# Seven-product block matmuls: partial sums kept in PSUM, remainders moved to VectorE, attention issued earlier

## The chip, the cores and the metric

The kernel runs on one core of a Trainium2 chip. The metric is device time in microseconds (us) of one launch. The core's engines are TensorE (PE in the profile; PEld is its weight load), VectorE (DVE), ScalarE (ACT), GpSimd (POOL) and SyncE (SP), which issues all of this kernel's transfers between HBM and the on-chip SBUF. TensorE writes its results only to PSUM, of which the kernel uses eight banks of 128 x 512 float32.

## The reference

An attention within chunks of 64 positions feeds two feed-forward layers, over 4608 tokens of width 512:

```python
scores = scale * q_c @ k_c.T            # 8 heads, chunks of 64 x 64
attn = softmax(scores); x = attn @ v_c  # -> (4608, 512)
g = x @ w_gate; val = x @ w_val         # 512 -> 1536 each
x = (g * sigmoid(g) * val) @ w_out      # 1536 -> 512
h = x @ w_in                            # 512 -> 2048
out = (h * sigmoid(1.702 * h)) @ w_out2 # 2048 -> 512
```

## The kernel before

**Tiling.** Tokens go in 9 blocks of 512 (NB = 9). The hidden columns of a layer are cut into passes: passes 0 and 1 hold six tiles of 128 columns each for layer 1, passes 2 and 3 eight tiles each for layer 2. A pass runs over all 9 blocks. Within a block the tiles of a pass come in groups: three groups of two tiles in passes 0 and 1 (27 groups a pass), two groups of four tiles in passes 2 and 3 (18 groups a pass); 90 groups in all.

**First matmuls.** A group multiplies with seven products instead of eight (the Strassen-Winograd scheme): sums and differences of quarters of the weights (`combos`) and of quarters of the block's tokens (`token_combos`) are made beforehand, and `group_products` adds and subtracts the seven results. Every float32 operand is held as a leading part and a remainder (`split`: ScalarE casts the leading part, another engine subtracts it for the remainder), so that each product of parts takes three matmuls (`mm3`). One product is 12 matmuls of 256 columns into one PSUM bank. Products are counted from 0. ScalarE copies the bank of product 0 (`copy(s1, m)`); VectorE adds the others into the sums with seven `tt` instructions, one each after products 1, 2, 3, 5 and 6 and two after product 4.

**Gate and second matmuls.** `gated` applies the sigmoid on ScalarE, multiplies on VectorE, and splits the result h into hh (cast on ScalarE) and hl (h minus hh; on GpSimd in pass 0, on VectorE after it). `second` multiplies hh and hl with a tile of the output weights, four quarters e = 0 to 3, three matmuls of 512 columns each, accumulated over the pass in four PSUM banks y0 to y3. A group's second matmuls wait in the list `pend` and are put between the products of the next group. `block_sum` adds a block's result to what earlier passes left in HBM.

**Pass 0** also makes the input: while it works on block b, `attend` computes the four attention units of block b + 1 (two sets of 32 small matmuls and four transposes on TensorE, reductions and the softmax on VectorE and ScalarE), and `x_made` turns their result xr (one buffer) into the seven token operands x (eight buffers, so all but one of the next block's wait for the last group of this block). Beside it the weights of pass 1 are unpacked and split (`group_to_dram`), mostly on GpSimd.

**Order.** The kernel writes out its own order: every instruction block is an `op` with an engine, an assumed duration and a priority (a planned time); `emit` plays this forward and, per engine, takes what could start first and, among those within 0.3 us (0.1 us on VectorE), the lowest priority. Each engine runs the resulting list in order and waits on semaphores for what an instruction needs. The plan assumes 1.2 us between the end of another engine's work and a TensorE instruction that needs it, and 0.3 us otherwise.

**PSUM.** Eight banks: y0 to y3; two of tag g, one s, one a. In pass 0 products alternate between the two g banks while s and a serve the attention; from pass 1 on products go round g, s, g, a.

Of the kernel before, what the change touches and what calls it, by code (L numbers as in the profile page):

```python
# [18 lines left out]
P = 128  # L19
# [120 lines left out]
def attention_two_moe_kernel(ctx: ExitStack, tc: tile.TileContext, q, k, v, wg, wv, wo, wi, wo2, out):  # L140
# [20 lines left out]

    nc = tc.nc
# [14 lines left out]
    FILL = 40  # L177
# [3 lines left out]
    for name, space in (("const", None), ("sb", None), ("ps", PSUM), ("dram", DRAM)):  # L181
        pool[name] = ctx.enter_context(tc.tile_pool(name=name, bufs=1, **({"space": space} if space else {})))
    ring = {tag: Ring(pool["sb"], tag, n) for tag, n in (
# [3 lines left out]
    ring.update({tag: Ring(pool["ps"], tag, n) for tag, n in (  # L187
        ("y0", 1), ("y1", 1), ("y2", 1), ("y3", 1), ("g", 2), ("s", 1), ("a", 1))})
# [53 lines left out]
    def mm3(o, ah, al, bh, bl, first, last):  # L242
        nc.tensor.matmul(o, ah, bh, start=first, stop=False)  # L243
        nc.tensor.matmul(o, ah, bl, start=False, stop=False)  # L244
        nc.tensor.matmul(o, al, bh, start=False, stop=last)  # L245
# [84 lines left out]
    def combos(t0, t1, prio):  # L330

        def half(i):
            return lambda ap: ap[:, i * 256:(i + 1) * 256]

        s1, s2, s3, s4 = [ring["st"].new([P, 256]) for _ in range(4)]
        a = half(0), half(1)
        yield t0, a[0]
        yield t0, a[1]
        tt(s1, t1, t1, ALU.add, 256, prio, "pool", a[0], a[1])
        tt(s2, s1, t0, ALU.subtract, 256, prio, "pool", of_b=a[0])  # L340
        yield s2, lambda ap: ap
        tt(s3, t0, t1, ALU.subtract, 256, prio, "pool", a[0], a[0])
        yield s3, lambda ap: ap
        yield s1, lambda ap: ap
        tt(s4, t0, s2, ALU.subtract, 256, prio, "pool", of_a=a[1])
        yield s4, lambda ap: ap
        yield t1, a[1]
# [77 lines left out]
    def attend(u, prio, load_prio, bufs=None, tags="sa"):  # L425
# [7 lines left out]
        s = ring[tags[0]].new([P, 512])  # L433

        def blocks(o, st, mv, of_o, of_st):

            for i in range(H):
                for r in (slice(0, CH), slice(CH, P)):
                    nc.tensor.matmul(o[r, of_o(i)], st[r, of_st(i)], mv[r, of_o(i)], start=True, stop=True)  # L439

        def cols(i):
            return slice(i * CH, i * CH + CH)

        op("pe", 1.2, lambda: blocks(s.ap, qb.ap, kb.ap, cols, cols), [qb, kb], [s], prio)
# [12 lines left out]

        pt = ring[tags[1]].new([P, 512])
# [8 lines left out]
        o = ring[tags[1]].new([P, 512])  # L467

        op("pe", 1.2, lambda: blocks(o.ap, vb.ap, e.ap, cols, cols), [vb, e], [o], prio)
        b = u // UPB  # L470
        if b not in xr:
            xr[b] = ring["xr"].new([P, KD, BT])
        ts = slice(u % UPB * P, u % UPB * P + P)
        copy(xr[b].part(lambda ap: ap[:, :, ts]), o, 512, prio, cut=lambda ap: ap.rearrange("p (a t) -> p a t", a=NP))


    def token_combos(xb, prio):
# [13 lines left out]
        return [(xb, b[0][0]), (xb, b[1][0]), (t2, same), (t3, same), (t1, same), (xb, b[1][1]), (t4, same)]  # L491
# [27 lines left out]
    m_tags = []  # L519

    def product(g, xs, i, prio):
        if not m_tags:
            m_tags.extend(["g", "g"] if prio < start[1][0] else ["g", "s", "g", "a"])
        m = ring[m_tags.pop(0)].new([P, 2, HT])
        w, x = W[g][i], xs[i]

        def fn():
            for var in range(2):
                for kk in range(2):
                    ks, cs = slice(kk * P, kk * P + P), kk  # L530
                    mm3(m.ap[:, var], w.ap[:, var, 0, ks], w.ap[:, var, 1, ks], x.ap[:, 0, kk], x.ap[:, 1, kk],
                        kk == 0, kk == 1)

        op("pe", GV, fn, [w, x], [m], prio)
        return m

    def group_products(g, xs, at, put):
# [4 lines left out]
        s1 = ring["s1"].new([P, 2, HT])  # L542
        u = ring["u"].new([P, 2, 2, HT])
        u2, u3 = [u.part(lambda ap, n=n: ap[:, n]) for n in range(2)]
        for i in range(7):
            at_i = at(i)
            m = product(g, xs, i, at_i)
            if i == 0:
                copy(s1, m, 512, at_i)
            elif i == 1:  # L550
                tt(q[0][0], s1, m, ALU.add, 512, at_i)
            elif i == 2:
                tt(u2, s1, m, ALU.add, 512, at_i)
            elif i == 3:
                tt(u3, u2, m, ALU.add, 512, at_i)
            elif i == 4:
                tt(q[0][1], u2, m, ALU.add, 512, at_i)
                tt(q[1][1], u3, m, ALU.add, 512, at_i)
            elif i == 5:
                tt(q[0][1], q[0][1], m, ALU.add, 512, at_i)  # L560
            else:
                tt(q[1][0], u3, m, ALU.subtract, 512, at_i)
            put(i)
        return c

    def gated(g, c, prio):

        hs = []
# [3 lines left out]
        for i, var in ([(0, 0), (1, 0)] if g.layer == 1 else [(i, var) for var in range(2) for i in range(2)]):  # L572
# [5 lines left out]
            if g.layer == 1:  # L578
# [4 lines left out]
                  h, 512, prio, "pool" if prio < start[1][0] else "dve")  # L583
            hs.append((hh, hl))
        return hs
# [50 lines left out]
    warm = ring["y0"].new([P, 512])  # L636

    def warm_up():
        for i in range(8):
            nc.tensor.matmul(warm.ap[:, :P], ident.ap, ident.ap, start=True, stop=True)  # L640

    op("pe", 3.6, warm_up, [ident], [warm], -99)
    for i in range(FILL):
        op("pe", 0.22, lambda: nc.tensor.matmul(warm.ap[:, :P], ident.ap, ident.ap, start=True, stop=True), [warm], [], 9999)
# [7 lines left out]
    for u in range(UPB):  # L652
# [4 lines left out]
        attend(u, -40 + 4 * u, -60 + u, bufs, (("s", "a"), ("g", "y2"), ("g", "y3"), ("y1", "y2"))[u])  # L657
# [4 lines left out]
    OW = {(0, 0, g0, 0): out_from_host(g0, 0, 0)}  # L662
    group_from_host(gs0[1], 2)
    for i in range(2):
        key = (0, 0, gs0[i], 1 - i)
# [18 lines left out]
    for p, (layer, gs) in enumerate(passes):  # L684
        jobs = spread(p)
        for b in range(NB):
# [3 lines left out]
            for j, g in enumerate(gs):  # L690
# [8 lines left out]
                c = group_products(g, xs, lambda i, tj=tj, step=step: tj + i * step / 7, put)  # L699
                if j == 0:  # L700
                    ys = [ring[f"y{e}"].new([P, BT]) for e in range(KD)]
                hs = gated(g, c, tj + step)
                for m, (hh, hl) in enumerate(hs):
                    for e in range(KD):
                        first, last = j == 0 and m == 0, j == len(gs) - 1 and m == len(hs) - 1

                        def fn(prio, g=g, m=m, hh=hh, hl=hl, e=e, first=first, last=last, ys=ys, p=p, b=b, layer=layer):
# [4 lines left out]
                            if last:  # L712
                                block_sum(p, b, ys, e, prio + 0.5)

# [63 lines left out]
```

## Time and profile before

| what | value |
|---|---|
| median of 3 runs | 1814.8 us (1814.05 to 1817.19) |
| profiled execution, its own time | 1817.76 us |
| its span, first to last instruction | 1815.7 us |
| TensorE busy in the span | 1745.7 us (96%) |
| VectorE, ScalarE, GpSimd busy | 1243.3, 703.7, 549.0 us |
| granted TensorE clock, mean share of full speed | 0.986 |

The profile comes from one execution. Matmuls overlap one another, so that a TensorE shown busy is not always one at its full rate; a stretch is better judged by how many matmuls it finished.

### The profile page before, as it was taken

The page shows a single profiled execution, that of the slowest core. Times are in us where ns is not written, and L with a number is a line of the kernel's source. Part 1 is how long each engine was busy: PE and PEld are TensorE (multiplying, and loading weights), DVE is VectorE, ACT ScalarE, POOL GpSimd, SP SyncE. Part 2 cuts the span into 40 slices and gives each one's busy share as a digit, 9 for nine tenths or more (in the row PEclk, how much of TensorE's full clock was granted, in tenths as well). Part 3 has the DMA queues.
Part 4 walks back from the last instruction along what each step waited for, and adds up shares of the span by engine and source line. Part 5 has one row for each costly group of instructions (what it writes and reads, how often), then busy time and mean ns, then how long its engine had stood idle before and what let it go on. Part 6 is the DMA issues. An engine that isn't in the chain of part 4 may idle for free.

```text
span 1815.7 us, 33814 instructions
## 1 busy us (share of the span) xinstructions
PE 1745.7 (96%) x13128; PEld 1581.0 (87%) x13128; DVE 1243.3 (68%) x1846; ACT 703.7 (39%) x1218; POOL 549.0 (30%) x594
## 2 busy tenths in 40 slices
PE   7869999998999999999999999999999999999998
PEld 7768888888988999999999998889888888888886
DVE  7988787888888567888888766555544455555554
ACT  5766455555554223333333233333222222222222
POOL 4775565566556033345434222200000000000000
PEclk9889999999999999999999999999999999999999
DMA  7457777777785988888888999966668667666664
GB/s 278 160 207 243 266 246 238 258 273 243 250 280 195 403 298 307 285 287 297 304 294 289 358 346 340 330 210 212 222 218 294 230 232 242 241 226 226 230 213 161
DMA packets 183918, 473.53 MB, mean 261 GB/s; under 512 B 19792, under 2 KB 46416, under 8 KB 183760
## 3 DMA queue, kind: packets, MB, share of 16 engines
q1 hardware_dynamic: 183760, 471.38, 75.4%
q8 instruction: 104, 1.70, 0.4%
q14 instruction: 54, 0.44, 0.1%
HBM read 336.56 MB, written 134.74 MB: 260 GB/s over the span
## 4 chain that ended last, share of the span: by engine, by line
PE 81%; DVE 9%; POOL 4%; issue 2%; DMA 2%; ACT 1%; SPq 0%; DVEq 0%; POOLq 0%; ACTq 0%
PE y L244 12%; PE y L243 12%; PE y L245 12%; PE g L243 9%; PE g L245 9%; PE g L244 9%; PE s L244 3%; PE s L245 3%; PE s L243 3%; PE a L244 3%; PE a L245 3%; PE a L243 3%; DVE h L236 2%; PE a L439 2%; DVE t L323 1%
## 5 line engine op out<-in xcount | busy, mean ns | idle before, releaser
L243 PE MATMUL g<-x,w 128*128 128x256 f32 x1640 | 470.3, 287 | 15.3 <-DVE c L236 7.5
L244 PE MATMUL g<-x,w 128*128 128x256 f32 x1640 | 465.6, 284 | 7.7 <-POOL x L236 7.4
L245 PE MATMUL g<-x,w 128*128 128x256 f32 x1640 | 465.0, 284 | 0.4 <-POOL w L236 0.4
L575 ACT ACTIVATE h<-c 128x512 f32<-128x512 f32 x252 | 156.6, 632 | 591.6 <-DVE c L236 585.5
L243 PEld LDWEIGHTS g<-x,w 128*128 128x128 f32 x1640 | 312.0, 190 | 33.0 <-DVE c L236 6.4
L244 PEld LDWEIGHTS g<-x,w 128*128 128x128 f32 x1640 | 311.8, 190 | 20.8 <-POOL x L236 9.0
L236 DVE TENSOR_TENSOR h<-h,c 128x512 f32<-128x512 f32 x360 | 289.1, 816 | 44.1 <-ACT h L575 40.3
L245 PEld LDWEIGHTS g<-x,w 128*128 128x128 f32 x1640 | 311.9, 190 | 0.6 <-POOL w L236 0.6
L227 ACT CAST hh<-h 128x512 fp32r<-128x512 f32 x252 | 154.5, 620 | 204.6 <-DVE h L236 100.8
L243 PE MATMUL y<-o,hh 128*128 128x512 f32 x576 | 227.6, 395 | 0.0
L245 PE MATMUL y<-o,hl 128*128 128x512 f32 x576 | 227.5, 395 | 0.0
L244 PE MATMUL y<-o,hh 128*128 128x512 f32 x576 | 227.3, 395 | 0.0
L236 DVE TENSOR_TENSOR hl<-h,hh 128x512 fp32r<-128x512 f32 x200 | 143.7, 726 | 70.1 <-ACT hh L227 68.4
L244 PE MATMUL y<-hl,o 128*128 128x512 f32 x432 | 173.7, 402 | 10.2 <-POOL hl L236 7.9
L243 PE MATMUL y<-hh,o 128*128 128x512 f32 x432 | 175.6, 407 | 4.4 <-ACT hh L227 4.4
L236 DVE TENSOR_TENSOR c<-u,g 128x512 f32<-128x512 f32 x174 | 114.2, 683 | 95.6 <-PE g L245 93.9
L245 PE MATMUL y<-hh,o 128*128 128x512 f32 x432 | 172.7, 400 | 0.0
L245 PEld LDWEIGHTS y<-o,hl 128*128 128x128 f32 x576 | 108.1, 188 | 26.1
L244 PE MATMUL s<-x,w 128*128 128x256 f32 x440 | 123.9, 282 | 0.0
L244 PE MATMUL a<-x,w 128*128 128x256 f32 x440 | 123.9, 282 | 0.0
L245 PE MATMUL s<-x,w 128*128 128x256 f32 x440 | 123.8, 281 | 0.0
L245 PE MATMUL a<-x,w 128*128 128x256 f32 x440 | 123.8, 281 | 0.0
(119 smaller groups left out, 3202.5 us busy)
## 6 DMA issues: line engine op xcount, KB each, us to landing
x<-x_dram SPq DMA_DIRECT2D x189, 512.0 KB, 5.6
o<-od_b SPq DMA_DIRECT2D x144, 512.0 KB, 4.9
o<-od_a SPq DMA_DIRECT2D x102, 512.0 KB, 5.3
x_dram<-x SPq DMA_DIRECT2D x63, 512.0 KB, 4.1
wd_b<-ws SPq DMA_DIRECT2D x56, 256.0 KB, 4.4
w<-wd_b SPq DMA_DIRECT2D x28, 512.0 KB, 6.3
raw<-in_moe_w_out SPq DMA_DIRECT2D x56, 255.8 KB, 4.1
wd_a<-ws SPq DMA_DIRECT2D x42, 256.0 KB, 4.1
```

What stands on the lines that cost most here:

```text
L227: op("act", act_us(n), lambda: nc.scalar.copy(out=dst.ap, in_=cut(src.ap)), [src], [dst], prio)
L236: lambda: e.tensor_tensor(out=dst.ap, in0=of_a(a.ap), in1=of_b(b.ap), op=by), [a, b], [dst], prio)
L243: nc.tensor.matmul(o, ah, bh, start=first, stop=False)
L244: nc.tensor.matmul(o, ah, bl, start=False, stop=False)
L245: nc.tensor.matmul(o, al, bh, start=False, stop=last)
L323: op("dve", dve_us(1.3 * n), lambda: nc.vector.scalar_tensor_tensor(out=t.ap.bitcast(I32), in0=t.ap, scalar=-4096 * up, in1=word(1).bitcas ...
L439: nc.tensor.matmul(o[r, of_o(i)], st[r, of_st(i)], mv[r, of_o(i)], start=True, stop=True)
L575: op("act", act_us(512), lambda h=h, i=i, var=var, by=by: nc.scalar.activation(out=h.ap, in_=of(var)(c[i].ap), func=AF.Sigmoid, scale=by), ...
```

## The change

Four things are changed together.

- `group_products` takes two PSUM banks for a group and issues some products on top of what stands in the bank: product 2 onto 0, product 4 onto 0 + 2, product 6 onto 3. The order of the products is changed (in `combos`, `token_combos`). ScalarE copies the bank after products 0, 2 and 4 (s1, u2, u3); VectorE adds or subtracts four times (after products 1, 4, 5 and 6). Product 2 must so wait until product 0 was read, and product 5, which overwrites the bank of product 4, until product 4 was copied. `pend` leaves room for second matmuls between products 4 and 5. In pass 0 all groups use banks ga and gb; later passes alternate with s and a.
- All remainders hl are subtracted on VectorE, in pass 0 too.
- The attention of the next block gets priorities that begin 22 us ahead of the block, 14 us apart (before: at the block's start, 12 us apart), and `x_made` 20 us ahead of its block (before: 12).
- Besides: y0 to y3 become two tiles ya, yb of two banks each; early attention units use other banks; `gated` takes the second half of the tokens first and makes a fourth h only when the first one's second matmuls are listed; the filler matmuls at the start go from 40 to 24.

```diff
-    FILL = 40
+    FILL = 24
-        ("w", 21), ("o", 3), ("x", 8), ("c", 3), ("s1", 1), ("u", 1), ("h", 2), ("hh", 3), ("hl", 3),
+        ("w", 21), ("o", 3), ("x", 8), ("c", 3), ("u", 3), ("h", 2), ("hh", 3), ("hl", 3),
-    ring.update({tag: Ring(pool["ps"], tag, n) for tag, n in (
-        ("y0", 1), ("y1", 1), ("y2", 1), ("y3", 1), ("g", 2), ("s", 1), ("a", 1))})
+    ring.update({tag: Ring(pool["ps"], tag, 1) for tag in ("ya", "yb", "ga", "gb", "s", "a")})
...
+        bank = [ring[t].new([P, 2, HT]) for t in (("s", "a") if p and n_groups[0] % 2 else ("ga", "gb"))]
...
+        for i, (k, goes_on) in enumerate(((0, 0), (1, 0), (0, 1), (1, 0), (0, 1), (0, 0), (1, 1))):
+            m, w, x = bank[k], W[g][i], xs[i]
...
+                            kk == var == 0 and not goes_on, kk == 1, skip_group_check=True)
...
             if i == 0:
                 copy(s1, m, 512, at_i)
             elif i == 1:
                 tt(q[0][0], s1, m, ALU.add, 512, at_i)
             elif i == 2:
-                tt(u2, s1, m, ALU.add, 512, at_i)
-            elif i == 3:
-                tt(u3, u2, m, ALU.add, 512, at_i)
+                copy(u2, m, 512, at_i)
             elif i == 4:
+                copy(u3, m, 512, at_i)
+                tt(q[1][1], u3, bank[1], ALU.add, 512, at_i)
+            elif i == 5:
+                tt(q[1][0], u3, m, ALU.subtract, 512, at_i)
+            elif i == 6:
                 tt(q[0][1], u2, m, ALU.add, 512, at_i)
-                tt(q[1][1], u3, m, ALU.add, 512, at_i)
-            elif i == 5:
-                tt(q[0][1], q[0][1], m, ALU.add, 512, at_i)
-            else:
-                tt(q[1][0], u3, m, ALU.subtract, 512, at_i)
...
-                  h, 512, prio, "pool" if prio < start[1][0] else "dve")
+                  h, 512, prio)
...
-        attend(u, -40 + 4 * u, -60 + u, bufs, (("s", "a"), ("g", "y2"), ("g", "y3"), ("y1", "y2"))[u])
+        attend(u, -40 + 4 * u, -60 + u, bufs, (None, None, "yb", "ya")[u])
...
-                    while len(pend) > n * (6 - i) // 7:
-                        pend.pop(0)(tj + (i + 0.5) * step / 7)
+                    while len(pend) > n * (7 - i - (i > 3)) // 8:
+                        pend.pop(0)(tj + (i + (i > 4) + 0.5) * step / 8)
...
-                        at = t + u * 12
+                        at = t - 22 + u * 14
...
-                        x_made(b + 1, start[p][b + 1] - 12)
+                        x_made(b + 1, start[p][b + 1] - 20)
```

## Rows read from the trace of the kernel before

**Rows 1.** The page's chain of work that ended last, by engine.

```profile
PE 81%; DVE 9%; POOL 4%; issue 2%; DMA 2%; ACT 1%; SPq 0%; DVEq 0%; POOLq 0%; ACTq 0%
```

**Rows 2.** Stages: start-up, pass 0 block 0, blocks 1-8, pass 1, passes 2-3.

```profile
core 0: us, PE busy (x) PEld busy (x) DVE busy (x) ACT busy (x) POOL busy (x), PEclk, DMA share, GB/s
0.00:34.50 34.50, 26.99 (x437) 25.26 (x437) 22.38 (x42) 17.80 (x33) 10.60 (x20) 0.97 0.78 283
34.50:125.30 90.80, 69.06 (x670) 61.13 (x669) 80.49 (x117) 65.05 (x126) 71.72 (x72) 0.84 0.52 183
125.30:616.60 491.30, 461.44 (x4334) 415.97 (x4333) 386.88 (x583) 265.00 (x433) 273.09 (x299) 0.99 0.75 258
616.60:1040.20 423.60, 421.56 (x2917) 391.56 (x2916) 344.67 (x479) 139.68 (x255) 158.34 (x157) 1.00 0.88 306
1040.20:1807.00 766.80, 766.66 (x4777) 687.11 (x4775) 407.55 (x627) 216.18 (x372) 35.30 (x48) 1.00 0.73 247
```

**Rows 3.** Same columns: one block of pass 1, one of pass 3.

```profile
663.30:709.90 46.60, 46.60 (x325) 43.49 (x324) 36.27 (x58) 17.45 (x32) 22.09 (x27) 1.00 0.86 287
1541.80:1584.10 42.30, 42.30 (x265) 37.94 (x264) 22.14 (x35) 10.62 (x19) 0.00 (x0) 1.00 0.69 235
```

**Rows 4.** TensorE's waits, blocks 1-8 of pass 0: total us, times, longest.

```profile
PE g L243 <- DVE c L236: 7.5, 7, 1.8
PE g L244 <- POOL x L236: 6.1, 5, 2.5
PE y L244 <- POOL hl L236: 5.3, 4, 1.9
PE y L243 <- ACT hh L227: 3.9, 4, 1.5
PE g L243 <- DVE u L236: 1.6, 2, 1.3
```

**Rows 5.** TensorE's waits in pass 1.

```profile
PE y L244 <- DVE hl L236: 2.0, 4, 0.6
```

**Rows 6.** VectorE by form, blocks 1-8 of pass 0: busy us, mean ns | idle before.

```profile
L236 DVE TENSOR_TENSOR h<-h,c 128x512 f32<-128x512 f32 x97 | 82.6, 866 | 8.6 <-ACT h L575 7.7
L236 DVE TENSOR_TENSOR c<-u,g 128x512 f32<-128x512 f32 x73 | 47.9, 682 | 29.8 <-PE g L245 29.6
```

**Rows 7.** VectorE by form, pass 1.

```profile
L236 DVE TENSOR_TENSOR hl<-h,hh 128x512 fp32r<-128x512 f32 x54 | 42.7, 790 | 0.7 <-ACT hh L227 0.3
```

**Rows 8.** VectorE by form, 1200 to 1800 us (passes 2 and 3, GpSimd idle).

```profile
L236 DVE TENSOR_TENSOR hl<-h,hh 128x512 fp32r<-128x512 f32 x115 | 77.9, 689 | 61.8 <-ACT hh L227 60.5
L236 DVE TENSOR_TENSOR h<-h,c 128x512 f32<-128x512 f32 x116 | 77.4, 688 | 16.4 <-ACT h L575 14.8
```

**Rows 9.** GpSimd by form, blocks 1-8 of pass 0.

```profile
L236 POOL TENSOR_TENSOR hl<-h,hh 128x512 fp32r<-128x512 f32 x48 | 67.1, 1405 | 97.5 <-ACT hh L227 95.7 <-issue 1.3
L236 POOL TENSOR_TENSOR x<-xr,x 128x512 fp32r<-128x512 f32 x29 | 42.7, 1481 | 1.4 <-DMA v<-in_v 1.2 <-ACT x L227 0.2
```

**Rows 10.** ScalarE by form, blocks 1-8 of pass 0.

```profile
L450 ACT ACT_TABLE_LOAD x22 | 28.2, 1283 | 0.4
...
L466 ACT COPY e<-a 128x512 f32<-128x512 f32 x27 | 15.7, 583 | 28.7 <-PE a L463 27.6 <-ACT h L575 0.6 <-DVE h L236 0.3
L227 ACT COPY s<-g 128x512 f32<-128x512 f32 x24 | 13.9, 579 | 5.8 <-PE g L245 5.7
```

**Rows 11.** Timeline, pass 0, a product that waits for a copy: start us, us.

```profile
128.31 0.66 PE L463 MATMUL a<-ident,e 128*128 128x128 f32 x4 [1.40 <-ACT xr L227]
...
130.00 0.28 PE L244 MATMUL g<-x,w 128*128 128x256 f32 x1
130.11 0.28 PE L245 MATMUL g<-x,w 128*128 128x256 f32 x1
130.24 0.58 ACT L227 COPY s<-g 128x512 f32<-128x512 f32 x1
...
130.87 0.39 PE L243 MATMUL g<-x,w 128*128 128x256 f32 x1 [0.48 <-ACT s L227]
```

**Rows 12.** Timeline of TensorE, an attention product of 32 small matmuls.

```profile
191.12 1.15 PE L439 MATMUL a<-e,v 64*64 64x64 f32 x32
192.20 0.39 PE L243 MATMUL g<-x,w 128*128 128x256 f32 x1
```

**Rows 13.** Timeline of TensorE in block 0, at a lower granted clock.

```profile
105.06 0.41 PE L244 MATMUL g<-x,w 128*128 128x256 f32 x1
105.27 0.41 PE L245 MATMUL g<-x,w 128*128 128x256 f32 x1
```

More of the change, by code (lines that the diff above doesn't have):

```diff
@@ L240, in split, with mm3 @@
         tt(lo, src, hi, ALU.subtract, n, prio, eng, of_a=cut, of_b=rd)
[L242 to L245, printed above, removed]
+    def mm3(o, ah, al, bh, bl, first, last, **kind):
+        nc.tensor.matmul(o, ah, bh, start=first, stop=False, **kind)
+        nc.tensor.matmul(o, ah, bl, start=False, stop=False, **kind)
+        nc.tensor.matmul(o, al, bh, start=False, stop=last, **kind)
     class Group:
@@ L432, in attend, with blocks @@
             load(b, src[u].rearrange("p h t -> p (h t)"), load_prio + 4 * (i > 1))
-        s = ring[tags[0]].new([P, 512])
-        def blocks(o, st, mv, of_o, of_st):
+        if both is None:
+            s = ring["s"].new([P, 512])
+        else:
+            both = ring[both].new([P, 2, 512])
+            s = both.part(lambda ap: ap[:, 0])
+        def blocks(o, st, mv):
             for i in range(H):
                 for r in (slice(0, CH), slice(CH, P)):
[L439 to L444, printed above, removed]
+                    cs = slice(i * CH, i * CH + CH)
+                    nc.tensor.matmul(o[r, cs], st[r, cs], mv[r, cs], start=True, stop=True)
+        op("pe", 1.2, lambda: blocks(s.ap, qb.ap, kb.ap), [qb, kb], [s], prio)
         m = ring["m"].new([P, H, 1])
@@ L456, in attend, with ps @@
             out=heads(e.ap), in0=heads(e.ap), in1=z.ap.to_broadcast([P, H, CH]), op=ALU.mult), [e, z], [e], prio)
-        pt = ring[tags[1]].new([P, 512])
+        def ps():
+            return ring["a"].new([P, 512]) if both is None else both.part(lambda ap: ap[:, 1])
+        pt = ps()
         def transposes():
@@ L466, in attend @@
         op("act", 0.59, lambda: nc.scalar.copy(out=e.ap, in_=pt.ap), [pt], [e], prio)
-        o = ring[tags[1]].new([P, 512])
-        op("pe", 1.2, lambda: blocks(o.ap, vb.ap, e.ap, cols, cols), [vb, e], [o], prio)
+        o = ps() if both is None else pt
+        op("pe", 1.2, lambda: blocks(o.ap, vb.ap, e.ap), [vb, e], [o], prio)
         b = u // UPB
@@ L490, in token_combos @@
         same = lambda ap: ap
-        return [(xb, b[0][0]), (xb, b[1][0]), (t2, same), (t3, same), (t1, same), (xb, b[1][1]), (t4, same)]
+        return [(xb, b[0][0]), (xb, b[1][0]), (t2, same), (t1, same), (t3, same), (t4, same), (xb, b[1][1])]
     X = {}
@@ L516, in x_to_dram, with group_products, fn @@
                 store(x_dram[1][:, b, i, c * 512:(c + 1) * 512], Buf(lambda s=s: s.ap.rearrange("p a t -> p (a t)"), None, None, s), [xd[1][b][i].part(None)], prio + i + 2)
[L519 to L537, printed above, removed]
+    n_groups = [0]
+    def group_products(g, xs, at, put, p):
+        n_groups[0] += 1
+        bank = [ring[t].new([P, 2, HT]) for t in (("s", "a") if p and n_groups[0] % 2 else ("ga", "gb"))]
         c = [ring["c"].new([P, 2, 2, HT]) for _ in range(2)]
         q = [[c[i].part(lambda ap, n=n: ap[:, n]) for n in range(2)] for i in range(2)]
[L542 to L545, printed above, removed]
+        s1, u2, u3 = [ring["u"].new([P, 2, HT]) for _ in range(3)]
+        for i, (k, goes_on) in enumerate(((0, 0), (1, 0), (0, 1), (1, 0), (0, 1), (0, 0), (1, 1))):
+            m, w, x = bank[k], W[g][i], xs[i]
+            def fn(m=m, w=w, x=x, goes_on=goes_on):
+                for var in range(2):
+                    for kk in range(2):
+                        ks = slice(kk * P, kk * P + P)
+                        mm3(m.ap[:, var], w.ap[:, var, 0, ks], w.ap[:, var, 1, ks], x.ap[:, 0, kk], x.ap[:, 1, kk],
+                            kk == var == 0 and not goes_on, kk == 1, skip_group_check=True)
             at_i = at(i)
-            m = product(g, xs, i, at_i)
+            op("pe", GV, fn, [w, x], [m], at_i)
             if i == 0:
@@ L566, in gated @@
     def gated(g, c, prio):
-        hs = []
         def of(var):
             return lambda ap: ap[:, :, var]
-        for i, var in ([(0, 0), (1, 0)] if g.layer == 1 else [(i, var) for var in range(2) for i in range(2)]):
+        for i, var in ([(1, 0), (0, 0)] if g.layer == 1 else [(i, var) for i in (1, 0) for var in range(2)]):
             h = ring["h"].new([P, 2, HT])
@@ L695, in put, with fn @@
                 def put(i, tj=tj, n=n, step=step):
-                    while len(pend) > n * (6 - i) // 7:
-                        pend.pop(0)(tj + (i + 0.5) * step / 7)
-                c = group_products(g, xs, lambda i, tj=tj, step=step: tj + i * step / 7, put)
+                    while len(pend) > n * (7 - i - (i > 3)) // 8:
+                        pend.pop(0)(tj + (i + (i > 4) + 0.5) * step / 8)
+                c = group_products(g, xs, lambda i, tj=tj, step=step: tj + (i + (i > 4)) * step / 8, put, p)
                 if j == 0:
-                    ys = [ring[f"y{e}"].new([P, BT]) for e in range(KD)]
-                hs = gated(g, c, tj + step)
-                for m, (hh, hl) in enumerate(hs):
+                    yab = [ring["y" + i].new([P, 2, BT]) for i in "ab"]
+                    ys = [yab[e // 2].part(lambda ap, e=e: ap[:, e % 2]) for e in range(KD)]
+                more, hs = gated(g, c, tj + step), []
+                hs.extend(next(more) for i in range(min(3, len(g.fs))))
+                for n in range(len(g.fs)):
                     for e in range(KD):
-                        first, last = j == 0 and m == 0, j == len(gs) - 1 and m == len(hs) - 1
-                        def fn(prio, g=g, m=m, hh=hh, hl=hl, e=e, first=first, last=last, ys=ys, p=p, b=b, layer=layer):
+                        first, last = j == 0 and n == 0, j == len(gs) - 1 and n == len(g.fs) - 1
+                        def fn(prio, g=g, n=n, hs=hs, more=more, e=e, first=first, last=last, ys=ys, p=p, b=b, layer=layer):
+                            m, hh, hl = hs[n]
                             key = (p, b, g, m)
@@ L713, in fn @@
                                 block_sum(p, b, ys, e, prio + 0.5)
+                            if e == KD - 1 and len(hs) < len(g.fs):
+                                hs.append(next(more))
                         pend.append(fn)
```

19 lines of the change are left out of this document (9 added, 10 removed).

## The prediction

> **What bounds the kernel now.** I read the chain of work that ended last, then a table of stages, then who TensorE waited for in each. The chain is TensorE's for 81% of the span, with VectorE at 9% and GpSimd at 4% [rows 1]; those 13% must lie somewhere in particular. The stages show where. In passes 2 and 3 TensorE is busy for 766.7 of 766.8 us, and in pass 1 for 421.6 of 423.6 [rows 2]. A block of pass 1 takes 46.6 us for its 324 matmuls, one of pass 3 takes 42.3 us for 264 [rows 3]; nine times 46.6 is 419.4, so pass 1 gives away about 4 us, and 18 times 42.3 is 761, so the last two passes give away almost nothing (the rest of their stretch is the second matmuls of the last group).
>
> Pass 0 is another matter. Blocks 1 to 8 take 491.3 us [rows 2]. Eight blocks of 46.6 are 372.8. An attention unit costs TensorE two products of 1.08 us (from the start of one to the start of what follows it) and transposes of at most 0.66 [rows 11, 12], some 2.6 with their overlap; 27 units, counted by their copies [rows 10], are 70. That is 443, so 48 us are lost there. TensorE is idle in 29.9 of them (491.3 - 461.4); the remaining 18 are slow restarts after a stop and matmuls at a lower clock, so that a microsecond of idle time costs about 1.6. In block 0, 21.7 us of 90.8 are idle at a clock of 0.84.
>
> So whatever the change does to VectorE in passes 1 to 3 can bring at most 4 us. What it can win lies in pass 0, and what it can lose lies in every pass, since there TensorE has no slack.
>
> **Sums in PSUM.** Each group loses three of seven VectorE additions and gains two ScalarE copies. At 0.682 us for an addition that reads PSUM [rows 6] and 0.579 for the copy [rows 10], the 24 groups of blocks 1 to 8 give VectorE back 72 x 0.682 = 49 us and cost ScalarE 48 x 0.579 = 28, on top of 265 of 491 (54%): it goes to about 64% of a shorter stretch.
>
> **Remainders on VectorE.** 48 subtractions leave GpSimd, which is relieved of 67 of 273 us [rows 2, 9]. On VectorE no row of pass 0 shows one. The bounds are 0.689 us, where GpSimd is idle [rows 8], and 0.866, what h x c with the same two SBUF inputs takes in pass 0 [rows 6]; pass 1 has this very instruction beside a working GpSimd at 0.790 [rows 7]. I take 0.83, nearer to pass 0's own row: 40 us. In return, 97 instructions h x c took 0.866 instead of 0.688 [rows 6, 8], 17 us of slowing beside a GpSimd busy for 56%; with a quarter less GpSimd work about 4 come back. VectorE's sum is -49 + 40 - 4 = -13: 374 us, in a stretch that I expect at about 466, so still 80%. The additions that read PSUM take 0.68 everywhere, so they aren't what GpSimd slows.
>
> The Trainium skill, "SBUF — State Buffer", section "Who interferes with whom", says that a VectorE instruction with two SBUF inputs and a GpSimd instruction that reads SBUF exclude each other for a whole instruction, whichever came first. The trace agrees in kind: 0.866 and 0.688 for the same form. If every moved subtraction stood behind one whole GpSimd instruction of 1.4 us, they would cost 67 us more and VectorE would have about 440 of 466 us to do; by the rows it is the 5 to 9 us already in the sum.
>
> **What this does to TensorE's waits in blocks 1 to 8** [rows 4]. For additions it waits 9.1 us (7.5 and 1.6) with two rotating banks. It keeps two banks, but a product now waits for one short reading instruction, half of the time on the less loaded ScalarE: I take 5 off (bounds 0 and 9). For x, made late on GpSimd at the change of block, 6.1: the attention is planned a third of a block earlier, and hl no longer stands between the x instructions of 1.48 us on GpSimd's queue: 5 off (0 and 6). For hl 5.3: VectorE needs 0.83 for GpSimd's 1.4 and has no queue of weight work ahead: 4 off (0 and 5). For hh 3.9: these fall where no product of the next block is ready, which an earlier x provides: 3 off (0 and 4). Together 17 of idle time, 27 us at 1.6. Against it stands the new direct wait of product 5 for the copy of product 4. A copy costs from the last matmul's start to the next product's start 130.87 - 130.11 = 0.76 us, where the next would have come after 0.12: 0.64 uncovered [rows 11]. By the new order two second matmuls stand in between. A product is 12 matmuls of 0.12, 1.42 us by the starts [rows 11]; 21 of them leave 16.8 of a block's 46.6 us for 24 second matmuls [rows 3], so one takes 0.70 and the two 1.4, and the wait is covered unless ScalarE is more than about 0.8 us late; a table load of 1.283 in front of it [rows 10] does that now and then. I charge 2 us. Blocks 1 to 8: -25 (bounds -48 and +10).
>
> **Block 0 and the start.** 6 subtractions less on a GpSimd that is busy for 71.7 of 90.8 us, three additions less per group on VectorE (80.5 of 90.8) [rows 2]. But two of the first four attention units now share the banks s and a one after the other, and the next block's first unit is planned ahead of this block's x. I take -3, between -10 and +8. Fewer fillers are priced at nothing: they fill idle time ahead of the first product; should the clock be lower when it starts, its 12 matmuls go at 0.21 us instead of 0.12 [rows 11, 13], 1 us a product.
>
> **Pass 1.** All its idle time, 2.0 us, is for hl behind a VectorE busy for 345 of 424 us [rows 2, 5]; 27 x 3 x 0.68 = 55 us less on VectorE: -2. **Passes 2 and 3:** nothing to win. The new wait is covered by four second matmuls (2.8 us) there, by two in pass 1: 0, at worst 63 x 0.64 = 40 us if nothing covers it. The two-bank tiles ya and yb make a block's first second matmul wait for two sums instead of one; a whole group of seven products (10 us) lies in between, which hides it. In the tail after 1807 us nothing changes.
>
> **Sum.** -25 - 3 - 2 = -30 us. The profiled execution's own time is 1817.8, so 1787.8; the median of the runs shown lies 3.0 under that execution, so 1784.8: I say 1785.
>
> **Rivals.**
>
> *VectorE stays the bound of pass 0.* It goes through its list in order, and each subtraction there now stands behind ScalarE's cast; additions that free a bank stand behind it. Then the 9.1 for additions and the 5.3 for hl remain, and only x and hh (8 us of idle time) are won: 8 x 1.6 = 13, with pass 1's 2: 1800. For it: 80% busy in order. Against it: in pass 1 VectorE is 81% busy with hl in its list, and TensorE idles 2.0 us in 27 groups.
>
> *The attention isn't moved in fact.* xr is a single buffer, so the first unit of the next block cannot deliver before this block's x is made, and it holds bank a till then. Then x is as late as now, hl's gain is partly taken by it, and -8 or less is left: 1808 to 1815, near no change.
>
> *Slower: TensorE stops before product 5.* The place is the same in every group: ScalarE copies product 4 late, and TensorE, without slack in passes 1 to 3, stops. Stopped fully in all 90 groups it costs 58 us: 1843; it decides from 30 / 90 = 0.33 us a group on, that is with ScalarE about 1.1 us late on average where two second matmuls cover. For it: 54% busy and, for the exponential alone, 22 table loads in blocks 1 to 8 [rows 10]. Against it: 140 of 424 and 216 of 767 us in the later passes [rows 2].
>
> *Slower by the clock.* If such stops let TensorE's clock fall in passes 1 to 3, one product of each group at 12 x 0.21 = 2.5 instead of 1.4 us is 63 x 1.1 = 69 us: about 1855. Blocks 1 to 8 had 30 us of idle time, with two banks, and still a clock of 0.99 [rows 2], which speaks against it. The Trainium skill, "TensorE: Matmul & The Clock Gate", section "A second HAM failure mode: psum-queue depth-cycling", tells of a kernel that cycled through PSUM banks and whose clock swung between the two levels for it; this trace does not show that for two banks.
>
> **How the numbers follow.** The forecast (1768 to 1803) gets 0.64, VectorE as the bound (1796 to 1811) 0.14, the attention not moved 0.06, the stop before product 5 0.12, the clock 0.04. A difference under 0.2% (3.6 us) can't be told from none. Faster: 0.64 + 0.14, and the third rival is split between faster and same: 0.79; same 0.05; slower 0.16. The range runs from 1762, where nearly all of the 48 us and block 0's 10 would come back (48 + 10 - 5), to 1818, which takes in the first three cases and leaves out most of the two slow ones, some 0.15; below 1762 I see 0.04.
>
> **What would show it.** Right: in the stages, blocks 1 to 8 near 466 us with VectorE near 374, ScalarE near 293 and GpSimd near 206 busy; TensorE's waits for x and hl there at a quarter; passes 2 and 3 at 42.3 us a block as now; hl on VectorE in pass 0 near 0.83. Wrong: TensorE waiting in its list for ScalarE's u in passes 1 to 3 (the stop), waits for VectorE's c and hl in pass 0 as long as now with VectorE above 85% (the bound), or the x row of the waits unchanged. A first product later than 34.5 us, or a block 0 longer than 91, would refute the small gain there.

## The result and the profile after

The changed kernel takes 1790.9 us (median of 4 runs, 1788.0 to 1791.9) against 1814.9 before: a ratio of 0.9863, with a 95% interval of 0.9846 to 0.9881. That is 24 us less where 30 were forecast, and it lies in the range. The profiled execution took 1788.0 us, the fastest of the four, and its span is 29.5 us shorter than before's. In one experiment below (four copies) one of four executions had a granted clock of 0.56 from its first microsecond to its last; it is left out of the numbers.

The stages of the changed kernel, with the borders set by the same events as in [rows 2] (first product, first product of block 1, of pass 1, of pass 2, last matmul):

```profile
core 0: us, PE busy (x) PEld busy (x) DVE busy (x) ACT busy (x) POOL busy (x), PEclk, DMA share, GB/s
0.00:39.60 39.60, 27.10 (x404) 25.07 (x405) 24.36 (x43) 21.96 (x43) 16.43 (x26) 0.84 0.68 246
39.60:129.20 89.60, 68.56 (x671) 60.93 (x669) 75.45 (x113) 62.34 (x123) 63.91 (x63) 0.86 0.54 190
129.20:589.90 460.70, 452.88 (x4330) 413.28 (x4331) 351.34 (x548) 281.30 (x469) 213.65 (x247) 1.00 0.80 276
589.90:1010.30 420.40, 420.40 (x2919) 391.74 (x2918) 280.84 (x409) 177.68 (x320) 168.27 (x174) 1.00 0.91 311
1010.30:1777.50 767.20, 767.18 (x4780) 687.98 (x4778) 335.40 (x516) 252.76 (x440) 27.64 (x33) 1.00 0.70 244
```

Read against [rows 2], in one profiled execution each: the first product comes 5.1 us later, block 0 is 1.2 shorter, blocks 1 to 8 are 30.6 shorter, pass 1 is 3.2 shorter, passes 2 and 3 are 0.4 longer, and the tail is the same. These add up to -29.5, the difference of the spans. TensorE's idle time in blocks 1 to 8 fell from 29.9 to 7.8 us. VectorE is busy 351 us there (374 forecast), ScalarE 281 (293), GpSimd 214 (206). The chain that ended last is now TensorE's for 90% of the span:

```profile
PE 90%; DVE 4%; ACT 1%; issue 1%; POOL 0%; DMA 0%; DVEq 0%; ACTq 0%; SPq 0%; POOLq 0%
```

TensorE's waits in blocks 1 to 8, all that are left of [rows 4]:

```profile
PE ga L244 <- ACT u L228: 5.3, 2, 3.1
PE ya L245 <- DVE hl L237: 1.6, 2, 0.9
PE ga L244 <- DVE c L237: 1.0, 1, 1.0
PE a L469 <- DVE e L458: 1.0, 1, 1.0
```

The waits for x and hh are gone. The new entry is the first: twice TensorE stood before product 5 until ScalarE had copied the bank (u). The longer of the two, in the timeline:

```profile
480.59 0.69 DVE L451 TENSOR_TENSOR e<-s,m 128x512 f32<-128x512 f32 x1
481.31 0.63 ACT L453 ACTIVATE e<-e 128x512 f32<-128x512 f32 x1 [6.12 <-DVE e L451]
481.85 0.57 ACT L228 COPY u<-ga 128x512 f32<-128x512 f32 x1
...
482.47 0.39 PE L244 MATMUL ga<-x,w 128*128 128x256 f32 x1 [3.11 <-ACT u L228]
```

ScalarE was idle for 6.12 us, held by an attention exponential at the head of its list, which waited for VectorE; the copy stood behind it. So the wait that was feared does occur, in pass 0, not because ScalarE is busy but because its list is in order. In the later passes the blocks take what they took [rows 3]:

```profile
636.60:683.30 46.70, 46.70 (x326) 43.52 (x325) 36.63 (x52) 21.80 (x41) 22.51 (x24) 1.00 0.89 295
1554.70:1597.00 42.30, 42.30 (x266) 37.98 (x265) 18.09 (x29) 12.71 (x23) 0.00 (x0) 1.00 0.67 238
```

The moved remainder costs VectorE less than the 0.83 taken, and the copy what [rows 10] said (first two rows VectorE, third ScalarE, blocks 1 to 8):

```profile
L237 DVE TENSOR_TENSOR h<-h,c 128x512 f32<-128x512 f32 x96 | 76.7, 822 | 3.2 <-ACT h L571 2.3
...
L237 DVE TENSOR_TENSOR hl<-h,hh 128x512 fp32r<-128x512 f32 x48 | 37.1, 778 | 0.5 <-ACT hh L228 0.4
```

```profile
L228 ACT COPY u<-ga 128x512 f32<-128x512 f32 x72 | 42.2, 586 | 59.9 <-PE ga L246 59.5
```

### The profile page after: what moved, and what is told of

The parts are those of the page before. It is cut to its first block, busy times and chain, and to the rows that moved or that the text cites. A ratio compares the mean times of both kernels' runs of the same rounds, so it can differ in the third digit from the quotient of the medians.

```text
span 1786.2 us, 33210 instructions
## 1 busy us (share of the span) xinstructions
PE 1736.1 (97%) x13096; PEld 1579.0 (88%) x13096; DVE 1068.7 (60%) x1628; ACT 796.0 (45%) x1392; POOL 489.9 (27%) x542
## 4 chain that ended last, share of the span: by engine, by line
PE 90%; DVE 4%; ACT 1%; issue 1%; POOL 0%; DMA 0%; DVEq 0%; ACTq 0%; SPq 0%; POOLq 0%
PE yb L244 6%; PE ya L245 6%; PE ya L244 6%; PE ya L246 6%; PE yb L246 6%; PE yb L245 6%; PE ga L244 6%; PE ga L246 6%; PE ga L245 6%; PE gb L244 4%; PE gb L246 4%; PE gb L245 4%; PE s L245 3%; PE s L246 3%; PE s L244 3%; PE a L246 2%
## 5 line engine op out<-in xcount | busy, mean ns | idle before, releaser
L237 DVE TENSOR_TENSOR h<-h,c 128x512 f32<-128x512 f32 x360 | 271.5, 768 | 39.2 <-ACT h L571 35.8
L244 PE MATMUL ga<-x,w 128*128 128x256 f32 x944 | 272.2, 288 | 19.1 <-ACT u L228 11.6
L246 PE MATMUL ga<-x,w 128*128 128x256 f32 x944 | 268.3, 284 | 0.7 <-POOL w L237 0.7
L245 PE MATMUL ga<-x,w 128*128 128x256 f32 x944 | 267.9, 284 | 0.0
L237 DVE TENSOR_TENSOR hl<-h,hh 128x512 fp32r<-128x512 f32 x252 | 187.6, 751 | 68.5 <-ACT hh L228 65.0
L228 ACT COPY u<-ga 128x512 f32<-128x512 f32 x177 | 103.5, 585 | 235.5 <-PE ga L246 235.1
L237 DVE TENSOR_TENSOR c<-u,gb 128x512 f32<-128x512 f32 x177 | 121.0, 684 | 142.9 <-ACT u L228 107.4
L244 PEld LDWEIGHTS ga<-x,w 128*128 128x128 f32 x944 | 179.6, 190 | 29.4 <-ACT u L228 13.0
L244 PE MATMUL gb<-x,w 128*128 128x256 f32 x708 | 202.3, 286 | 0.0
L245 PE MATMUL gb<-x,w 128*128 128x256 f32 x708 | 201.0, 284 | 0.4 <-POOL x L237 0.4
L246 PE MATMUL gb<-x,w 128*128 128x256 f32 x708 | 201.3, 284 | 0.0
L245 PEld LDWEIGHTS ga<-x,w 128*128 128x128 f32 x944 | 179.9, 191 | 6.7
L246 PEld LDWEIGHTS ga<-x,w 128*128 128x128 f32 x944 | 179.8, 191 | 1.2 <-POOL w L237 1.2
L246 PE MATMUL s<-x,w 128*128 128x256 f32 x496 | 139.8, 282 | 0.0
L245 PE MATMUL s<-x,w 128*128 128x256 f32 x496 | 139.5, 281 | 0.0
L244 PE MATMUL s<-x,w 128*128 128x256 f32 x496 | 139.2, 281 | 0.0
L245 PEld LDWEIGHTS gb<-x,w 128*128 128x128 f32 x708 | 135.2, 191 | 4.0 <-POOL x L237 0.6
L244 PEld LDWEIGHTS gb<-x,w 128*128 128x128 f32 x708 | 135.2, 191 | 3.9
L246 PEld LDWEIGHTS gb<-x,w 128*128 128x128 f32 x708 | 135.1, 191 | 0.0
L237 DVE TENSOR_TENSOR c<-u,a 128x512 f32<-128x512 f32 x93 | 63.6, 684 | 117.7 <-ACT u L228 109.9
```

What stands on the lines that cost most here:

```text
L228: op("act", act_us(n), lambda: nc.scalar.copy(out=dst.ap, in_=cut(src.ap)), [src], [dst], prio)
L237: lambda: e.tensor_tensor(out=dst.ap, in0=of_a(a.ap), in1=of_b(b.ap), op=by), [a, b], [dst], prio)
L244: nc.tensor.matmul(o, ah, bh, start=first, stop=False, **kind)
L245: nc.tensor.matmul(o, ah, bl, start=False, stop=False, **kind)
L246: nc.tensor.matmul(o, al, bh, start=False, stop=last, **kind)
```

## Which part brought it: seven kernels

The change has three parts: sums in PSUM (S), hl on VectorE in pass 0 (H), attention and x earlier (A). S here carries all the smaller edits that the section on the change lists under "Besides" (two-bank y tiles, other banks for the first attention units, the order in `gated`, fewer fillers); but for the banks, tried further below, no run takes these apart from the sums. Each alone and each pair was run, each beside runs of the kernel before on the same chip. Every one of these kernels has its own written-out order, so that a difference of a few us between two of them can be the order's. Theory 1 was that the change of block decides (x late, GpSimd shared by x and hl), theory 2 that VectorE's load does.

| parts | median us | ratio to before, 95% interval |
|---|---|---|
| S | 1816.5 | 1.0008 (0.9999 to 1.0018) |
| A | 1796.9 | 0.9898 (0.9883 to 0.9912) |
| H | 1796.2 | 0.9889 (0.9873 to 0.9906) |
| S + H | 1803.5 | 0.9936 (0.9918 to 0.9954) |
| S + A | 1793.5 | 0.9882 (0.9865 to 0.9898) |
| A + H | 1790.2 | 0.9861 (0.9843 to 0.9879) |
| S + A + H, the change | 1790.9 | 0.9863 (0.9846 to 0.9881) |

**S alone** is the changed kernel with these three edits undone:

```diff
-                  h, 512, prio)
+                  h, 512, prio, "pool" if prio < start[1][0] else "dve")
-                        at = t - 22 + u * 14
+                        at = t + u * 12
-                        x_made(b + 1, start[p][b + 1] - 20)
+                        x_made(b + 1, start[p][b + 1] - 12)
```

> The changed kernel with two parts undone: hl on GpSimd in pass 0 and the old priorities of the attention; only the sums in PSUM are left. Theory 1 (the gain comes from the change of block: x earlier and GpSimd free of hl): VectorE loses about 49 us of additions in blocks 1 to 8, but the waits for x and hl stay, so little of the 24 us is won: 1800 to 1812. Theory 2 (VectorE's load is what set pass 0): most of the gain is here, 1785 to 1795. Either way pass 1 keeps its 3 us, since nothing there differs from the changed kernel.

Measured 1816.5: the part that gave the change its name brings nothing by itself. VectorE's busy time in blocks 1 to 8 fell, as it should, and the stage did not get shorter; pass 1 kept its 3 us (420.2 against 423.6):

```profile
124.80:618.00 493.20, 465.66 (x4331) 421.40 (x4331) 342.47 (x514) 293.99 (x488) 288.99 (x318) 0.97 0.77 266
```

342 us of VectorE instead of 387, and 493 us instead of 491. What TensorE waited for in that stage is x, on both engines that make it, and c:

```profile
PE ga L245 <- POOL x L237: 8.3, 6, 2.0
PE ga L244 <- ACT x L228: 5.8, 5, 2.0
PE gb L244 <- DVE c L237: 5.7, 5, 2.0
```

Theory 2 falls: relief for VectorE alone was not worth anything while x was late. And in this order x is later than before: GpSimd ends the last of its seven x instructions 14 to 15 us after the block's first product at the last five of the eight changes of block, where the kernel before has two such changes (14.0 and 14.8 us; these times are read off the timelines). So this run does not show what the sums would be worth with x on time; the pairs below do.

**A alone** puts the two priorities of the change into the kernel before.

> The kernel before with the new priorities of the attention and of x alone. Theory 1: x is ready at the change of block, its wait of 6.1 us and the wait for hh of 3.9 go, hl stays on GpSimd: 1798 to 1806, with the first product later than 34.5 us if the early attention is what delays it. Theory 2: VectorE still has all additions, nothing is won: 1812 to 1818.

Measured 1796.9, 18 us less, more than theory 1 gave it. Blocks 1 to 8 took 471 us. No wait for x, hh or hl is left. The waits for additions that free a bank are 11.4 us, where they were 9.1 (7.5 and 1.6) [rows 4]:

```profile
PE g L243 <- DVE u L236: 11.4, 5, 2.9
PE a L463 <- DVE e L455: 2.6, 2, 1.8
PE g L243 <- ACT s L227: 2.4, 1, 2.4
```

**H alone** is one line in the kernel before:

```diff
-                  h, 512, prio, "pool" if prio < start[1][0] else "dve")
+                  h, 512, prio)
```

> The kernel before with hl on VectorE in pass 0 alone. Theory 1 (x late at the change of block is what counts first): x still ends 8 to 15 us after the block has begun, so at most the 5.3 us of idle time for hl are won: 1806 to 1814. Theory 2 (VectorE's load counts by itself): 38 us more on VectorE without fewer additions make it slower: 1820 to 1830. By the prediction's terms alone it is 4 x 1.6 = 6 us, near 1809.

Measured 1796.2, 20 us less: both theories missed it, and so did the prediction's 6 us for hl. Its stage of blocks 1 to 8:

```profile
123.90:596.40 472.50, 458.56 (x4333) 415.77 (x4332) 382.17 (x618) 257.10 (x419) 208.06 (x237) 0.99 0.78 263
```

VectorE has 48 subtractions more there (and 13 conversions of packed weights fewer, which fell into other stages), and its busy time went down, from 387 to 382 us. Over the whole kernel it stayed where it was, 1243.3 and 1243.8 us. Two groups show why:

```profile
L236 DVE TENSOR_TENSOR hl<-h,hh 128x512 fp32r<-128x512 f32 x48 | 37.5, 789 | 1.6 <-ACT hh L227 1.4
L326 DVE SCALAR_TENSOR_TENSOR t<-raw,t 128x256 int32<-128x256 int32 x56 | 31.8, 571 | 0.7
```

and the second of them before, in the same stage:

```profile
L326 DVE SCALAR_TENSOR_TENSOR t<-raw,t 128x256 int32<-128x256 int32 x63 | 46.8, 745 | 0.6
```

The moved subtractions cost 37.5 us, and the unpacking of weights, which also reads two SBUF tiles, fell from 745 to 571 ns each once 67 us of GpSimd work with such reads were gone. It is so in all eight kernels: this instruction takes 712 to 746 ns in the four with hl on GpSimd and 571 to 619 ns in the four with hl on VectorE. The prediction had allowed 4 us for this, on h x c alone. TensorE's waits in that stage (no wait for x is left):

```profile
PE y L244 <- DVE hl L236: 8.4, 8, 1.8
...
PE g L243 <- DVE c L236: 0.4, 1, 0.4
```

The wait that bears H's name grew, from 5.3 to 8.4 us, and the 9.1 us for additions fell to 0.4, though H changes no addition. And x itself: GpSimd at a change of block before (the new block's first product started at 435.54),

```profile
436.65 1.70 POOL L236 TENSOR_TENSOR x<-xr,x 128x512 fp32r<-128x512 f32 x1
438.32 1.74 POOL L236 TENSOR_TENSOR hl<-h,hh 128x512 fp32r<-128x512 f32 x1
441.34 1.29 POOL L236 TENSOR_TENSOR hl<-h,hh 128x512 fp32r<-128x512 f32 x1 [1.28 <-ACT hh L227]
442.58 1.30 POOL L236 TENSOR_TENSOR x<-xr,x 128x512 fp32r<-128x512 f32 x1
...
449.03 1.28 POOL L236 TENSOR_TENSOR x<-xt,x 128x512 fp32r<-128x512 f32 x1
```

with H alone (first product at 307.87),

```profile
303.68 3.33 POOL L236 TENSOR_TENSOR x<-xr,x 128x512 fp32r<-128x512 f32 x2 [0.65 <-ACT x L227]
...
312.91 1.74 POOL L236 TENSOR_TENSOR x<-xt,x 128x512 fp32r<-128x512 f32 x1
```

Before, hl's two instructions stood between the first and the second x, the second of them waiting 1.28 us for its cast, and x was held up behind them. The last x was there 14.8 us after its block had begun (450.31 - 435.54), with H alone 6.8 (314.65 - 307.87). The first is the worst of the eight changes of block. Over all eight the last x came 0.4 to 14.8 us after the first product before (some 7 us or more at six of them), 5.0 to 6.8 with H alone, and at most 1.6 us after it with A alone and 0.5 in the changed kernel. Of TensorE's waits in the stage before, 27.9 of 29.6 us lie between 10 us ahead of a block's first product and 15 us after it. H takes hl out of GpSimd's queue; A has x done before. Both remove the waits for x, so their gains do not add. Beyond that they differ: with A the waits for hh and hl go and those for additions stay; with H those for hl stay and those for additions go. Why the latter go is not shown.

**The pairs.** S + H (the change without A), S + A (without H) and A + H (without S):

> The changed kernel with the attention and the making of x at their old priorities; sums in PSUM and hl on VectorE stay. Theory 1: TensorE waits for x again at the change of block and 8 to 13 us of the 31 won in blocks 1 to 8 are lost, though the first product may come back to 34.5 us (5 us earlier): 1792 to 1800. Theory 2: blocks 1 to 8 stay near 461 us, and only the start changes: 1784 to 1790.

> The changed kernel with hl back on GpSimd in pass 0; the sums and the early attention stay. Theory 1: GpSimd has 67 us more to do, x and hl share its queue, and waits for hl (5.3 us of idle time before) come back: 1795 to 1802. Theory 2: VectorE has 37 us less to do in blocks 1 to 8, and the time is the same or lower: 1783 to 1792.

> The kernel before with the early attention and hl on VectorE, but with the old sums. Theory 1 (with x in time TensorE's next wait is for the additions that free a bank, 11.4 us of idle time for u in the run with the early attention alone, and hl on VectorE adds to what stands in front of them): blocks 1 to 8 at 470 to 480 us, no better than with the early attention alone, 1795 to 1803; the sums are then worth 7 us or more although they were worth nothing alone. Theory 2 (the parts add): hl brings 4 us on top of the early attention, 1791 to 1794.

S + H took 1803.5 (1798.1 to 1811.0, seven runs), just above theory 1's bounds, and worse than H alone: the intervals 0.9918 to 0.9954 and 0.9873 to 0.9906 do not meet. In its profile, the slowest of the seven runs, no wait for x is left either, but the waits for additions are back (7.6 us); whether the sums or merely the other order does that is open. S + A took 1793.5, just above theory 2's bounds and below theory 1's: with x early, GpSimd's hl hurts little. A + H took 1790.2, just under theory 2's bounds (7 us less than A alone, where H alone had brought 20), and as fast as the whole change. Its waits in blocks 1 to 8 are those that S was to remove:

```profile
PE g L243 <- DVE u L236: 9.5, 4, 3.5
PE g L243 <- DVE c L236: 2.4, 2, 1.3
```

In the changed kernel 1.0 us of them is left, and it has 5.3 us for ScalarE's copies in their place. So S, with the small edits that it carries, changes who is waited for, saves 3 us in pass 1, and leaves the whole time where it was: 1790.2 without, 1790.9 with it. Part of what it loses lies at the start: with other banks for the first attention units (below) the kernel with S takes 1782.4 us (A + H was not run with another start). Where the rest goes in pass 0 cannot be read off: two profiles of one and the same pass 0 (the changed kernel and the next experiment, which differs from pass 1 on) gave 460.7 and 464.8 us for blocks 1 to 8, so stages of single profiles that differ by some 4 us tell nothing.

## The direct wait of product 5, measured

The copy of product 4's bank was executed twice, then four times, in passes 1 to 3, where TensorE has no slack; the plan, and so the order, stayed the same:

```diff
                 copy(u3, m, 512, at_i)
+                if p:
+                    slow, fn0 = prog.ops[-1], prog.ops[-1].fn
+                    slow.fn = lambda fn0=fn0: [fn0() for _ in range(2)]
```

> The changed kernel with the copy of product 4's bank executed twice in passes 1 to 3 (63 groups), unknown to the plan, which orders the instructions as before. It makes the direct wait of product 5 longer by 0.58 us. Theory 1 (the wait is covered by the second matmuls that the plan puts between, with about 0.8 us to spare): passes 1 to 3 stay at 46.7 and 42.3 us a block, the time stays within 2 us. Theory 2 (the wait is just met, and any lateness of ScalarE shows): 0.3 to 0.58 us a group, 20 to 37 us more, near 1820.

> The changed kernel with the copy of product 4's bank executed four times in passes 1 to 3, unknown to the plan: 1.75 us more in front of product 5. With one extra copy nothing was lost. By the plan's allowance (2.1 us from product 4's end, of which the single copy needs about 0.8) some 1.3 us are spare, so 0.4 to 0.5 us are uncovered: 63 x 0.4 to 0.5 = 25 to 32 us more, near 1818, with TensorE waiting for u in passes 1 to 3. If it loses less than 10 us, the second matmuls in between cover more than the plan counts; if more than 60 us, ScalarE's other work is pushed late as well.

Two copies: 1790.1 us (1788.2 to 1790.8), the same as one. Passes 2 and 3 took the same 767.2 us with 20 us more ScalarE work:

```profile
1012.70:1779.90 767.20, 767.20 (x4781) 688.01 (x4779) 334.18 (x516) 273.36 (x476) 28.47 (x33) 1.00 0.71 244
```

Four copies: 1802.4, 1806.5 and 1806.8 us, some 16 more than the changed kernel, half of what was expected. Spread over 63 groups that would be 0.25 us each, so on average about 1.5 of the 1.75 us added are covered, where the prediction had given the wait 0.8 of room. Product 4's last matmul and product 5's first in a group of pass 1 of the changed kernel show where it comes from:

```profile
679.65 0.28 PE L246 MATMUL s<-x,w 128*128 128x256 f32 x1
...
681.86 0.28 PE L244 MATMUL s<-x,w 128*128 128x256 f32 x1
```

From start to start 2.21 us, which is three second matmuls in place of the two that the priorities ask for (the plan's allowance for a TensorE instruction that waits for ScalarE makes it take another); less the 0.76 that the copy needs, 1.45 are spare. The room is not the same everywhere: 18 of the 27 groups of pass 1 have these 2.2 us and 8 have 4.3, and in passes 2 and 3 nearly all have 2.9 or more, the four second matmuls that the prediction counted. By that list only some 19 groups would lose anything to four copies, 0.3 us each and 6 us in all (an estimate: 1.75 + 0.76 - 2.21 each). Where the other 10 us are lost is not shown.

## The start

The first product came at 39.6 us instead of 34.5. TensorE's list just ahead of it, in the changed kernel:

```profile
38.88 1.09 PE L469 MATMUL a<-ident,e 128*128 128x128 f32 x4 [2.95 <-DVE e L458]
39.62 0.56 PE L244 MATMUL ga<-x,w 128*128 128x256 f32 x1
```

and in the kernel before:

```profile
33.70 1.09 PE L463 MATMUL a<-ident,e 128*128 128x128 f32 x4 [2.52 <-ACT w L227]
34.49 0.58 PE L243 MATMUL g<-x,w 128*128 128x256 f32 x1
```

The next block's attention (the first row of each) stands ahead of the first product in both kernels, so it is not new. What is later is x: VectorE begins to make it at 32.8 us instead of 29.1. Two edits, alone and together:

```diff
-                        at = t - 22 + u * 14
+                        at = t - 22 + u * 14 if b else t + u * 12
```

> The changed kernel, but with the old priorities for the attention that runs within block 0 alone (later blocks keep the early ones). Theory 1 (the first product comes 5 us later because TensorE's and VectorE's lists hold the second block's attention ahead of it): the first product is back near 35 us, block 0 stays near 90, time 1785 to 1788. Theory 2 (the first four units are late because two of them share the banks s and a): the first product stays at 39 to 40 us, the time is 1789 to 1794.

```diff
-        attend(u, -40 + 4 * u, -60 + u, bufs, (None, None, "yb", "ya")[u])
+        attend(u, -40 + 4 * u, -60 + u, bufs, (None, "yb", "ya", None)[u])
```

> The changed kernel with other banks for the first four attention units: the second and third get the y banks, and the fourth shares s and a with the first. Theory 1 (the next block's attention in front): no change, first product at 39 to 40 us, 1789 to 1794. Theory 2 (two units one after the other in s and a): the second unit no longer waits, the first product comes 2 to 4 us earlier, 1786 to 1789.

> Both of the two edits at the start together: old priorities for the attention within block 0 and the other banks for the first four units. By either theory the first product comes at 34 to 36 us and the time is 1784 to 1788, the lowest so far; if it stays at 39 us, what delays the start is neither, and the transfers or the weights are left.

The old priorities in block 0 gave 1786.6 (0.9838, interval 0.9823 to 0.9852, which still touches the changed kernel's), with the first product at 35.9 us as theory 1 had it. But that is one matmul; the next waits for x:

```profile
35.95 0.58 PE L244 MATMUL ga<-x,w 128*128 128x256 f32 x1 [1.79 <-ACT x L228]
39.54 0.58 PE L245 MATMUL ga<-x,w 128*128 128x256 f32 x1 [3.01 <-DVE x L237]
```

The second matmul of the changed kernel comes at 39.98 us. So this edit hardly moved the start, and theory 1's reason is not borne out; what the run wins, it wins later in block 0 (85.5 us). The other banks gave 1782.4 (0.9813, 0.9799 to 0.9828, clear of the changed kernel), with the first product at 37.6, its second matmul at 38.0, and a block 0 shorter by 5.7 us:

```profile
37.60:121.50 83.90, 66.30 (x670) 57.27 (x668) 70.89 (x113) 61.09 (x121) 62.53 (x62) 0.90 0.60 205
```

Both together gave 1790.5, no gain: the first product came at 35.0 us, but again with one matmul, and the second at 39.7. Block 0, counted from 35.0, took 92.3 us. TensorE waits there 4.3 us for that x and most for VectorE's work on the next block's attention:

```profile
PE a L469 <- DVE e L458: 7.7, 2, 4.5
```

So the start waits for x on VectorE; the other banks alone brought it forward, by 2 us, and what block 0 takes depends on the whole new order.

**The fastest version.** On top of the other banks, the plan was given for two unpacking instructions the durations they have beside GpSimd:

```diff
-        op("dve", dve_us(1.3 * n), lambda: nc.vector.scalar_tensor_tensor(
+        op("dve", dve_us(1.9 * n), lambda: nc.vector.scalar_tensor_tensor(
-        op("dve", dve_us(1.4 * n), lambda: nc.vector.scalar_tensor_tensor(
+        op("dve", dve_us(1.8 * n), lambda: nc.vector.scalar_tensor_tensor(
```

> The changed kernel with the other banks for the first attention units (1782.4 us) and, in the plan alone, the two conversion instructions on VectorE counted at 0.66 and 0.63 us as they take beside GpSimd, instead of 0.50 and 0.53. Theory 1 (the two long waits for u in pass 0 stand behind an exponential that waits for VectorE, late by its conversions): the order adapts and up to 5 us of idle time in blocks 1 to 8 go: 1774 to 1781. Theory 2 (those waits are chance results of one order): another order with other waits, 1780 to 1790.

It took 1783.1 (0.9821, 0.9806 to 0.9835): theory 2, no gain. The version with the other banks alone, at 1782.4, beats both kernels.

## Why the prediction was right, and where it was not

- *The bound.* Passes 2 and 3 had nothing to win or lose, pass 1 gave 3.2 us (2 forecast), and pass 0 all the rest: right.
- *Blocks 1 to 8: -25 forecast, -30.6 in the profile.* The total was near, its terms were not. They were read as separate waits [rows 4] and added: x and hh 8 us of idle time (13 us), hl 4 (6 us), additions 5 (8 us). The runs show A alone at -18, H alone at -20, S alone at 0, and A + H at -26. The prediction did say that hl stands between the x instructions on GpSimd's queue; what it missed is that A and H each remove the waits for x alone. The step that failed is to take the size of a cure from the wait that bears its name: with H the wait for hl grew (5.3 to 8.4 us), while those for x and for additions went. That the sum came out near is luck in part: A + H gave more than the 19 us priced for x, hh and hl, and the sums nothing of their 8. A stage profiled again with the same pass 0 gave -26.5.
- *1.6 us for each us of idle time.* Blocks 1 to 8 lost 22.1 us of idle time and got 30.6 shorter, 1.4 each; with H alone 16.0 and 18.8, 1.2 each.
- *The sums.* -8 for fewer additions was wrong: 0 alone, and no gain on top of A + H. The 9.1 us of waits for additions were gone with H alone, which has every addition, and were 11.4 with A alone; on top of A + H the sums remove most of them, but put waits for copies in their place.
- *VectorE's load.* 374 us forecast, 351 measured. The moved subtractions cost 37 us (40 forecast); what GpSimd's reads cost VectorE was sized at 4 us on one form and was larger, on the unpacking above all (745 ns before, 619 in the changed kernel), and 8 unpackings fewer fell into the stage. The Trainium skill, "SBUF — State Buffer", section "Who interferes with whom", says that a VectorE instruction with two SBUF inputs contends with a GpSimd instruction that reads SBUF; the 745 against 571 ns with H alone agree.
- *Product 5.* Covered in passes 1 to 3, as said, with more room than 0.8 us: three second matmuls stand there in most groups of pass 1, not two. The 2 us charged in pass 0 came out as 5.3 us of idle time, in two places, behind an exponential and not a table load.
- *Block 0 and the start: -3 forecast, +3.9 measured.* The first product came 5.1 us late. Of the two risks named there the shared banks came true (2 us of it come back without them); the next block's attention stood ahead of the first product before as well. The other 3 us lie in the making of x, which VectorE begins and ends later; why is open.
- *The rivals.* VectorE did not stay the bound in the changed kernel (1.0 us for c, 1.6 for hl). The attention did move: the last x is there when its block begins. No stop and no lower clock in passes 1 to 3: no wait of TensorE stands there, and the clock is 1.00.

## What to carry to other kernels

When several waits cluster at one place, look for the one queue that they share before pricing them apart; two cures of one queue need not add. Relief for a busy engine (here VectorE, 45 us) can bring nothing while the wait that ends last is elsewhere: run each part of a change alone. Under an order written out in advance every edit makes a new order, and here such orders moved the start-up by several us either way, so an edit there has to be timed and not argued.

## What the runs showed of the hardware that was not expected

Moving some 50 subtractions of 0.79 us each to VectorE left its busy time over the whole kernel where it was (1243.8 us against 1243.3), since its other instructions with two SBUF inputs became shorter (the unpacking from 745 to 571 ns) once GpSimd no longer did the subtractions. In this kernel GpSimd's work was paid twice, in its own queue and on VectorE.
